# A fused attention and spectral-mix kernel: early y sums a tile sooner, a repeated x product, and moved Q jobs

## The chip, the cores and the metric

The kernel runs on one core of a Trainium2 chip. The time is device microseconds of one execution; the value given for a kernel is the median of several runs. Engines are named as in the profile: PE (TensorE matmul), PEld (its weight load), DVE (VectorE), ACT (ScalarE), POOL (GpSimd), SP (SyncE, which issues the output DMAs).

## The reference

First a causal attention with a forgetting gate, over 8 batches, 8 heads, 576 positions and 64 values per head. Its output x (8 x 576 x 512) then goes through a spectral mix with 64 modes, whose weights are by far the largest input:

```
X = rfft(x, axis=1)[:, :64]
Yr = Xr @ w_r[m] - Xi @ w_i[m]          # a 512x512 matrix for each mode m
Yi = Xr @ w_i[m] + Xi @ w_r[m]
y = irfft(Y, n=576, axis=1)
u = x + y
out = u + relu(u @ w_ch)
```

## The kernel before

The mode weights come in 64 tiles of about 1 MB (`emit_w_load`, L92), through POOL's DMA queue into a ring of nine buffers `wb` (NRING, L57). `emit_modes(n)` (L119) multiplies tile n: 32 products of 16 columns for the tiles of the second half, into a PSUM tile `A`; a DVE add (L163) then puts the sum with what the first half left in `Yacc` into `YTe` (early modes) or `YTl` (late modes). Tiles 32 to 47 hold the modes of `YTe`, the last sixteen (GL, L81) those of `YTl`.

While the weights stream, attention runs first. Then `u @ w_ch` is split: `XW = x @ w_ch` (`emit_xw`, L741) needs no mode. From tile 48 on the early half of y is complete, and is added to x and XW in 40 **parts** (a list of pairs, four for each pair of batches bp and more: one `emit_y(bp)`, L767, then nine `emit_part`, L772). `emit_y` transposes YTe of a batch pair on PE (L710), copies it on DVE (L715), multiplies it by w_ch in eight products (L718) and copies that on ACT (L726). `emit_part` forms x plus early y in `pu` and XW plus its early y in `pz` on PE (`add`, L728, four to six matmuls of 512 columns, all at L729), and evacuates them back to `x_all` and `XW`: on DVE two casts of 64 rows (L794, L795) or one whole cast (L790), on ACT two casts (L796, L797, or L792). PSUM at that time is a pool of six banks `psBig` (L737) and two for `A`.

The loop at L805 emits tile after tile, and behind each the parts that its rule at L814 makes due. `nmode` there is the number of tiles emitted, so with 15 as divisor all 40 parts are out behind tile 62, the last but one (tiles count from 0 to 63). The order in which the engines get these instructions is not quite the emitted one: the framework's scheduler places them by its own estimate, and adds the waits.

After the loop the PSUM pools are replaced by `psZ` (L820), four tiles of two banks; a tile of it waits for what used its banks before. Then the **output jobs** run (list at L881 to L885): for each pair of batches four jobs of two row blocks and one half job, 20 in all. `emit_x` (L845) puts x and XW into the job's `pu` and `pz` with products with a 64x64 identity, eight matmuls of 64x512 in the four corners of the PE array; `emit_out` (L852) adds the late y's products to them, copies `pu` on ACT (L859), and then, by the job's type, for N does relu and add in one DVE instruction (L864), for Q does the relu on ACT (L861) and the add on POOL (L862). The result goes out by a DMA from SP's queue (L874, or L870 for the half job). `emit_late(bp)` (L828) prepares the late y of a batch pair with `y_rows`, as `emit_y` does for the early one (L710, L715, L718, L726), with one psZ tile `pl`. The order is: x products of job 0, tile 63, late y of pair 0, then the jobs, with the late y of the next pair behind jobs 2, 7 and 12.

Of the kernel before, what the change touches and what calls it, by code (L numbers as in the profile page):

```python
# [11 lines left out]
ALU = mybir.AluOpType  # L12
# [9 lines left out]
def kernel(  # L22
# [11 lines left out]
    nc = tc.nc  # L34
    B, H, S, Dh = q.shape
    NM = moe_w_r.shape[0]
    D = H * Dh
# [14 lines left out]
    def xi(b, sb):  # L52
        return (b % 2) * 3 + sb if sb < 3 else 6 + b % 2 if sb == 3 else 8
# [14 lines left out]
    ident_bf = const.tile([128, 128], BF16, name="ident_bf")  # L68
# [9 lines left out]
    NT = NDC * NG  # L78
    NTH = NT // 2
    M2 = MG // 2  # L80
    GL = 16  # L81
# [92 lines left out]
    with ExitStack() as actx:  # L174
# [176 lines left out]
        for r0, n in RG:  # L351
# [7 lines left out]
            for h in range(2):  # L359
                hs = slice(h * 64, h * 64 + 64)  # L360
# [281 lines left out]
        nmode = 0  # L642

        def next_w():
            nonlocal nload
            if nload < NDC * NG:
                emit_w_load(nload)
                nload += 1
# [38 lines left out]
    with ExitStack() as bctx:  # L687
# [40 lines left out]
        def add(p, lhsT, rhs, first):  # L728
            nc.tensor.matmul(  # L729
                p, lhsT=lhsT, rhs=rhs, start=first, stop=not first, skip_group_check=True  # L730
            )

        with ExitStack() as cctx:
            late["psM"] = cctx.enter_context(
                tc.tile_pool(name="psM2", bufs=2, space=bass.MemoryType.PSUM)
            )
            psBig = cctx.enter_context(  # L737
                tc.tile_pool(name="psBig", bufs=6, space=bass.MemoryType.PSUM)
            )

            def emit_xw(n):  # L741
                bp, i0, nb = n // 2, (0, 5)[n % 2], (5, 4)[n % 2]
                xT = xTs[n % 3]
                for eb in range(NDC):
                    ptr = psBig.tile([128, SP], BF16, tag="big", name="ptr")
                    for i in range(nb):
                        nc.tensor.transpose(
                            ptr[:, i * 128 : (i + 1) * 128],
                            x_all[:, bp, i0 + i, eb * 128 : (eb + 1) * 128],
                            ident_bf[:, :],  # L750
                        )
                    nc.vector.tensor_copy(  # L752
                        xT[:, eb, 0 : nb * 128], ptr[:, 0 : nb * 128]
                    )
                for i in range(nb):
                    pxw = psBig.tile([128, D], F32, tag="big", name="pxw")
                    for eb in range(NDC):
                        nc.tensor.matmul(  # L758
                            pxw[:, :],
                            lhsT=xT[:, eb, i * 128 : (i + 1) * 128],  # L760
                            rhs=wch[:, eb, :],
                            start=(eb == 0),
                            stop=(eb == NDC - 1),
                        )
                    nc.scalar.copy(XW[:, bp, i0 + i, :], pxw[:, :])  # L765

            def emit_y(bp):  # L767
                pyw = psBig.tile([128, D], F32, tag="big", name="pyw")
                yp = psBig.tile([128, D], BF16, tag="big", name="yp")
                y_rows(YTe, 0, bp, yp[:, :], pyw[:, :])  # L770

            def emit_part(b, sb):  # L772
                pu = psBig.tile([128, D], F32, tag="big", name="pu0")
                pz = psBig.tile([128, D], F32, tag="big", name="pz0")
                bp, h = b // 2, b % 2
                xs, zs = x_all[:, bp, xi(b, sb), :], XW[:, bp, xi(b, sb), :]
                for t, (p, src) in enumerate(((pu, xs), (pz, zs))):
                    add(p[:, :], ident_bf[:, :], src, True)
                    for k in range(2 if sb == 4 else 1):
                        half = (b + k + t) % 2  # L780
                        add(
                            p[HS[k], :] if sb == 4 else p[:, :],
                            (BI if half else BIx)[
                                HS[half], sb * 128 : (512 + 64 if sb == 4 else sb * 128 + 128)
                            ],
                            yy[HS[half], 0, bp, t, :],
                            False,
                        )
                if sb == 4:
                    nc.vector.tensor_copy(xs, pu[:, :])  # L790
                    for k in range(2):
                        nc.scalar.copy(zs[HS[1 - k]], pz[HS[k], :])  # L792
                    return
                nc.vector.tensor_copy(xs[HS[h]], pu[HS[0], :])  # L794
                nc.vector.tensor_copy(zs[HS[h]], pu[HS[1], :])  # L795
                nc.scalar.copy(xs[HS[1 - h]], pz[HS[0], :])  # L796
                nc.scalar.copy(zs[HS[1 - h]], pz[HS[1], :])  # L797

            parts = []
            for bp in range(B // 2):  # L800
                parts += [(bp, None)]
                parts += [(b, sb) for b in (2 * bp, 2 * bp + 1) for sb in range(4)]
                parts += [(2 * bp, 4)]
            nx = done = 0
            while nmode < NT - 1:  # L805
                emit_modes(nmode)
                nmode += 1
                next_w()
                if nmode > NTH + 6 and nmode % 4 and nx < B:
                    emit_xw(nx)  # L810
                    nx += 1
                if nmode > NT - GL:
                    assert nx == B
                    while done < (nmode - NT + GL) * len(parts) // (GL - 1):  # L814
                        a, sb = parts[done]
                        emit_y(a) if sb is None else emit_part(a, sb)
                        done += 1
            assert done == len(parts)
# [13 lines left out]
        def pieces(job):  # L832
            b, sb, nb, _ = job
            for i in range(nb):
                at = b // 2, xi(b, sb + i)
                for k in range(2):
                    for t in range(2):
                        half = (b + t + (k if sb == 4 else 0)) % 2
                        src = (x_all, XW)[t if sb == 4 else k]
                        c0 = 512 if sb == 4 else (sb + i) * 128 + HM * k  # L840
                        yield t, i, HS[k], HS[half], src[HS[half], at[0], at[1], :], (
                            BIx if half else BI
                        )[HS[half], c0 : c0 + HM]

        def emit_x(job):  # L845
            pu = psZ.tile([128, 2, D], F32, tag="z", name="pu")
            pz = psZ.tile([128, 2, D], F32, tag="z", name="pz")
            for t, i, o, hs, src, _ in pieces(job):
                add((pu, pz)[t][o, i, :], ident_bf[hs, hs], src, True)
            return pu, pz  # L850

        def emit_out(job, ps, last):  # L852
            b, sb, nb, ty = job
            for t, i, o, hs, _, basis in pieces(job):
                add(ps[t][o, i, :], basis, yy[hs, 1, b // 2, t, :], False)
            pu, pz = (p[:, 0:nb, :] for p in ps)
            uo = wpool.tile([128, 2, 2, D], F32, tag="wb", name="uo")
            u_sb, o_sb = uo[:, 0, 0:nb, :], uo[:, 1, 0:nb, :]
            nc.scalar.copy(u_sb, pu)  # L859
            if ty == "Q":  # L860
                nc.scalar.activation(o_sb, pz, ACT.Relu)  # L861
                nc.gpsimd.tensor_tensor(o_sb, o_sb, u_sb, ALU.add)  # L862
            else:
                nc.vector.scalar_tensor_tensor(  # L864
                    o_sb, pz, 0.0, u_sb, ALU.max, ALU.add
                )
            if sb == 4:
                for h in range(2):
                    eng = nc.scalar if last and h else nc.sync
                    eng.dma_start(  # L870
                        out[b + h, 512:576, :], uo[64 * h : 64 * h + 64, 1, 0, :]
                    )
            else:
                nc.sync.dma_start(  # L874
                    out[b, 128 * sb : 128 * sb + 256, :].rearrange(
                        "(p r) e -> p r e", r=2
                    ),
                    o_sb,
                )

        jobs = []  # L881
        for bp in range(B // 2):
            jobs += [(b, sb, 2) for b in (2 * bp, 2 * bp + 1) for sb in (0, 2)]
            jobs.append((2 * bp, 4, 1))
        jobs = [(*j, ty) for j, ty in zip(jobs, "NNQNNNNQNNNNQNNNNNNN")]  # L885
        ps0 = emit_x(jobs[0])
        emit_modes(nmode)
        emit_late(0)
        for n, job in enumerate(jobs):
# [31 lines left out]
```

## Time and profile before

| | |
|---|---|
| median of 6 runs | 455.24 us (452.23 to 458.49) |
| the profiled execution | 456.33 us, its span 454.6 us |
| granted PE clock, mean over the span | 0.808 of full |
| PE busy | 384.6 us, 85% |
| DVE busy | 276.7 us, 61% |
| ACT busy | 245.7 us, 54% |
| POOL busy | 129.4 us, 28% |
| DMA | 97.02 MB, mean 213 GB/s |

The profile is of one execution. Its time is the span plus 1.7 us outside it, so times inside the span can be set against 456.33; the median of the runs shown is 1.1 us below that execution. A busy share is an average over stages with different limits, and PE also counts as busy while its matmuls run at a lower clock. All places in the profile are in us from the start of the span.

### The profile page before, as it was taken

Reading aid. Unit: us, or ns where it says so; the run is one execution under the profiler, and the core shown is the slowest. Engines: PE = TensorE matmul, PEld = TensorE weight load, DVE = VectorE, ACT = ScalarE, POOL = GpSimd, SP = SyncE. Lnnn points to the kernel's source line nnn. Section 1 sums busy time; section 2 is a strip of 40 time slices with the busy share of each in tenths; the row PEclk is TensorE's granted clock in tenths of the full one; section 3 lists DMA queues with packets and bytes.
Section 4 is the critical chain, followed back from the end, with each engine's and each line's share of the span. In section 5 each row is a group of like instructions: output and inputs, shape, how many; then the busy total and the mean of one; then the engine's idle time right before and its main releaser. Section 6 shows DMA issues by size and latency. Waiting matters only on the chain.

```text
span 454.6 us, 11981 instructions
## 1 busy us (share of the span) xinstructions
PE 384.6 (85%) x5134; PEld 247.7 (54%) x5149; DVE 276.7 (61%) x671; ACT 245.7 (54%) x372; POOL 129.4 (28%) x191
## 2 busy tenths in 40 slices
PE   2797798999887886987879886999999999979883
PEld 1464666776666565666656665666654433324341
DVE  5677778876455655555665776243359758393454
ACT  3787477774444636436446381334447764563663
POOL 7333331333323323233231213332323222000320
PEclk9996699996566858556755598899999985796998
DMA  9999999999999999999999999999999999911667
GB/s 197 222 236 260 210 255 217 222 223 212 236 211 236 236 210 237 233 214 236 234 214 211 212 210 188 209 211 211 213 210 211 211 211 211 211 20 59 244 246 286
DMA packets 49748, 97.02 MB, mean 213 GB/s; under 512 B 3296, under 2 KB 12128, under 8 KB 49696
## 3 DMA queue, kind: packets, MB, share of 16 engines
q0 software_dynamic: 46240, 85.93, 96.8%
q1 hardware_dynamic: 3376, 10.21, 6.1%
q8 instruction: 40, 0.66, 0.5%
q10 hardware_dynamic: 80, 0.13, 0.1%
q14 instruction: 12, 0.10, 0.1%
HBM read 163.73 MB, written 9.44 MB: 381 GB/s over the span
## 4 chain that ended last, share of the span: by engine, by line
PE 42%; DMA 17%; ACT 14%; DVE 11%; issue 4%; POOL 0%; ACTq 0%; DVEq 0%
DMA wb<-in_moe_w_i_dram 17%; PE pav L554 8%; ACT E L516 8%; PE A L147 7%; PE ps L509 6%; PE tp L457 5%; PE pz L729 4%; PE pu L729 3%; PE px L597 2%; DVE QTs L472 2%; PE vp L481 2%; ACT KT L470 2%; ACT uo L859 2%; DVE uo L864 2%; DVE XT L611 1%
## 5 line engine op out<-in xcount | busy, mean ns | idle before, releaser
L516 ACT ACTIVATE E<-ps 128x1024 bf16<-128x1024 f32 (+1 forms) x128 | 101.6, 854 | 29.0 <-PE ps L509 19.2
L90 POOL DMA_DIRECT2D wb<-in_moe_w_r_dram x65 | 43.3, 667 | 142.0 <-PE A L147 50.9
L147 PEld LDWEIGHTS <-wb 128*128 128x128 bf16 x2048 | 66.1, 100 | 23.2 <-issue 16.1
L147 PE MATMUL A<-XT,wb 128*128 128x16 bf16 x2048 | 73.0, 181 | 5.6 <-DVE Yacc L158 1.8
L509 PE MATMUL ps<-QTs,KT 64*128 64x64 bf16 (+4 forms) x384 | 59.0, 332 | 15.1 <-ACT E L516 13.7
L90 POOL DMA_DIRECT2D wb<-in_moe_w_i_dram x65 | 43.3, 666 | 68.7 <-DMA wb<-in_moe_w_i_dram 30.4
L554 PE MATMUL pav<-va,E 128*128 128x65 bf16 (+1 forms) x1088 | 58.2, 216 | 4.1 <-DVE x_all L576 3.5
L554 PEld LDWEIGHTS <-E 128*128 128x128 bf16 (+1 forms) x1088 | 48.0, 119 | 19.5 <-issue 8.3
L531 DVE TENSOR_TENSOR E<-E,trimask 128x256 bf16<-128x256 bf16 (+2 forms) x128 | 37.1, 301 | 19.6 <-ACT E L516 19.2
L474 ACT COPY VT<-tp 128x640 bf16<-128x640 bf16 (+1 forms) x32 | 23.3, 755 | 33.5 <-PE tp L457 33.2
L765 ACT CAST XW<-pxw 128x512 bf16<-128x512 f32 x36 | 20.8, 586 | 35.4 <-PE pxw L758 35.2
L509 PEld LDWEIGHTS <-KT 64*128 64x128 bf16 x384 | 19.5, 100 | 30.5 <-issue 21.7
L758 PE MATMUL pxw<-wch,yy 128*128 128x512 bf16 x133 | 34.1, 387 | 0.8 <-DVE yy L752 0.2
L470 ACT COPY KT<-tp 128x640 bf16<-128x640 bf16 (+1 forms) x32 | 22.1, 755 | 21.9 <-PE tp L457 21.9
L472 DVE COPY QTs<-tp 128x640 bf16<-128x640 bf16 (+1 forms) x32 | 23.2, 766 | 14.3 <-PE tp L457 14.2
L729 PEld LDWEIGHTS <-ident_bf 64*64 64x64 bf16 (+1 forms) x216 | 14.1, 104 | 32.0 <-issue 27.5
L794 DVE CAST x_all<-pu 64x512 bf16<-64x512 f32 x32 | 21.8, 682 | 15.8 <-PE pu L729 15.0
L864 DVE SCALAR_TENSOR_TENSOR uo<-pz,uo 128x1024 f32<-128x1024 f32 (+1 forms) x17 | 18.4, 1097 | 18.8 <-ACT uo L859 18.8
L576 DVE TENSOR_TENSOR x_all<-pav,rcp 128x384 bf16<-128x384 f32 x64 | 29.1, 454 | 0.8
L796 ACT CAST x_all<-pz 64x512 bf16<-64x512 f32 x32 | 18.5, 578 | 20.4 <-PE pz L729 19.0
L565 DVE RECIPROCAL rcp<-pav 128x6 f32<-128x6 f32 x64 | 12.1, 189 | 27.4 <-PE pav L554 26.4
L729 PE MATMUL pu<-x_all,ident_bf 64*64 64x512 bf16 (+1 forms) x72 | 26.2, 407 | 3.0 <-ACT uo L859 2.1
(119 smaller groups left out, 620.2 us busy)
## 6 DMA issues: line engine op xcount, KB each, us to landing
wb<-in_moe_w_r_dram POOLq DMA_DIRECT2D x63, 512.0 KB, 16.2
wb<-in_moe_w_i_dram POOLq DMA_DIRECT2D x63, 512.0 KB, 16.9
stv<-in_v_dram POOLq DMA_DIRECT2D x15, 576.0 KB, 15.1
out_dram<-uo SPq DMA_DIRECT2D x16, 512.0 KB, 2.8
stk<-in_k_dram POOLq DMA_DIRECT2D x16, 288.0 KB, 15.3
stq<-in_q_dram POOLq DMA_DIRECT2D x16, 288.0 KB, 15.2
out_dram<-uo SPq DMA_DIRECT2D x7, 128.0 KB, 3.2
stv<-in_v_dram SPq DMA_DIRECT2D x1, 576.0 KB, 4.3
```

The source lines that it names most:

```text
L90: tc.keep_in_program_order(nc.gpsimd.dma_start(dst, src))
L147: nc.tensor.matmul(A[:, eb, mi, :], lhsT=w_of(mi, eb * 128), rhs=x_of(m), start=(i == 0), stop=(i == len(terms) - 1),)
L470: nc.scalar.copy(rows(KTs[pr % 2][:, :, 0:S]), tv)
L472: nc.vector.tensor_copy(rows(QT[pr][:, :, :]), tv)
L509: nc.tensor.matmul(ps[:, b, o : o + n], lhsT=KTs[pr % 2][bs, h, jb * 128 : (jb + 1) * 128], rhs=QT[pr][bs, h, jb * 128 + c0 : jb * 128 + c ...
L516: nc.scalar.activation(E[:, :, piece * 512 : piece * 512 + w], ps[:, :, 0:w], ACT.Exp, scale=scale,)
L531: nc.vector.tensor_tensor(dg, dg, tr, ALU.mult)
L554: nc.tensor.matmul(pav[64 * half : 64 * half + w, slot, :], lhsT=E[:, b, c : c + (w - 1) * st + 1 : st], rhs=va[:, jb, b, :], start=(n == ...
L576: nc.vector.tensor_tensor(xo, pi, ri, ALU.mult)
L729: nc.tensor.matmul(p, lhsT=lhsT, rhs=rhs, start=first, stop=not first, skip_group_check=True)
L758: nc.tensor.matmul(pxw[:, :], lhsT=xT[:, eb, i * 128 : (i + 1) * 128], rhs=wch[:, eb, :], start=(eb == 0), stop=(eb == NDC - 1),)
L864: nc.vector.scalar_tensor_tensor(o_sb, pz, 0.0, u_sb, ALU.max, ALU.add)
```

## The change

Three edits and one addition. The parts rule divides by 14 instead of 15, so that all 40 parts are out behind tile 61. `emit_x` gets a count, and job 0's x product is emitted four times over into the same PSUM tiles, each time from the start. The Q jobs are 5, 10 and 15 instead of 2, 7 and 12. A new type D (relu and add on DVE straight from PSUM, without the ACT copy) is written into `emit_out`; no job in the list has it.

```diff
-                    while done < (nmode - NT + GL) * len(parts) // (GL - 1):
+                    while done < min(len(parts), (nmode - NT + GL) * len(parts) // (GL - 2)):
                         a, sb = parts[done]
                         emit_y(a) if sb is None else emit_part(a, sb)
                         done += 1
...
-        def emit_x(job):
+        def emit_x(job, times=1):
             pu = psZ.tile([128, 2, D], F32, tag="z", name="pu")
             pz = psZ.tile([128, 2, D], F32, tag="z", name="pz")
-            for t, i, o, hs, src, _ in pieces(job):
-                add((pu, pz)[t][o, i, :], ident_bf[hs, hs], src, True)
+            for _ in range(times):
+                for t, i, o, hs, src, _ in pieces(job):
+                    add((pu, pz)[t][o, i, :], ident_bf[hs, hs], src, True)
             return pu, pz
...
-            nc.scalar.copy(u_sb, pu)
-            if ty == "Q":
+            if ty != "D":
+                nc.scalar.copy(u_sb, pu)
+            if ty == "D":
+                nc.vector.scalar_tensor_tensor(o_sb, pz, 0.0, pu, ALU.max, ALU.add)
+            elif ty == "Q":
                 nc.scalar.activation(o_sb, pz, ACT.Relu)
                 nc.gpsimd.tensor_tensor(o_sb, o_sb, u_sb, ALU.add)
...
-        jobs = [(*j, ty) for j, ty in zip(jobs, "NNQNNNNQNNNNQNNNNNNN")]
-        ps0 = emit_x(jobs[0])
+        jobs = [(*j, ty) for j, ty in zip(jobs, "NNNNNQNNNNQNNNNQNNNN")]
+        ps0 = emit_x(jobs[0], 4)
         emit_modes(nmode)
         emit_late(0)
```

## The prediction

> **What bounds the kernel now.** First the page's busy tenths in 40 slices of 11.4 us, to see which stage is limited by what.
>
> ```profile
> PE   2797798999887886987879886999999999979883
> ...
> PEclk9996699996566858556755598899999985796998
> DMA  9999999999999999999999999999999999911667
> ```
>
> The DMA row is full for 35 slices: the weights set the time until the last tile lands. The windows view has 91 GB/s in 398 to 400 us and 5 GB/s after, so it lands at about 399. Yet the span is 454.6: 55 us follow, and the change works there. Next, the timeline from the fourth pair's early y to the last tile's product (start, duration, engine, line; in brackets the idle time before it and its releaser).
>
> ```profile
> 396.33 0.68 DVE L794 CAST x_all<-pu 64x512 bf16<-64x512 f32 x1 [5.00 <-PE pu L729]
> ...
> 408.52 0.69 DVE L790 CAST x_all<-pu 128x512 bf16<-128x512 f32 x1
> ...
> 408.64 0.37 PE L729 MATMUL pz<-x_all,ident_bf 64*64 64x512 bf16 x1 [2.60 <-DVE XW L795]
> ...
> 409.27 0.99 PE L147 MATMUL A<-XT,wb 128*128 128x16 bf16 x32
> ```
>
> The last tile's product starts at 409.27, ten us after its weights are there. What it waits for is DVE's queue of evacuations, unbroken from 396.33 to 409.21: eight parts at 1.44 us (two casts), two YTl adds at 0.40, one whole cast. DVE began late because PE was late, and that was the clock (columns: PE, PEld, DVE, ACT, POOL busy, granted clock, DMA share, GB/s):
>
> ```profile
> 372.00:373.00 1.00, 1.00 (x3) 0.13 (x2) 0.00 (x0) 0.63 (x2) 0.00 (x0) 0.51 1.15 215
> 392.00:393.00 1.00, 1.00 (x6) 0.11 (x2) 0.00 (x0) 0.25 (x1) 0.00 (x0) 0.75 1.13 211
> ...
> 409.00:410.00 1.00, 0.99 (x35) 0.81 (x29) 0.21 (x1) 0.00 (x0) 0.00 (x0) 0.78 0.00 0
> 416.00:417.00 1.00, 1.00 (x12) 0.60 (x8) 0.76 (x1) 0.21 (x1) 0.00 (x0) 0.80 0.00 0
> ```
>
> Read as fractions of a us, the clock halves at 372.02, returns at 392.50, halves at 409.56 and returns at 416.40: steps of 20.48, 17.06 and 6.84, which are 6, 5 and 2 times 3.41. Each fall comes 1.1 us (0.9 for the second) after a PE pause: 1.21 us for a weight tile (369.71 to 370.92), 2.6 us above. A part's matmuls then step by 0.54 us (376.38, 376.93) instead of 0.32 (345.25, 345.57).
>
> Last, ACT's timeline in one group of five output jobs, and the chain there.
>
> ```profile
> 424.62 1.01 ACT L859 COPY uo<-pu 128x1024 f32<-128x1024 f32 x1 [1.11 <-PE pz L729]
> 426.00 1.01 ACT L859 COPY uo<-pu 128x1024 f32<-128x1024 f32 x1 [0.38 <-PE pz L729]
> 428.00 1.01 ACT L859 COPY uo<-pu 128x1024 f32<-128x1024 f32 x1 [0.99 <-PE pz L729]
> 428.91 1.03 ACT L861 ACTIVATE uo<-pz 128x1024 f32<-128x1024 f32 x1
> 429.94 0.58 ACT L726 CAST yy<-pl 128x512 bf16<-128x512 f32 x1
> ```
> ```profile
> 412.31 1.85 PE pl L718 x8
> ...
> 428.91 0.98 PE pl L718 x8
> ```
>
> Jobs 5, 6 and 7 are copied at 424.62, 426.00, 428.00; 7 is the Q job, with its relu at 428.91. The group repeats every 8.96 us (422.00, 430.92, 439.93). No engine is full in it: PE, ACT and DVE hand on two pairs of PSUM tiles. The late y's eight products end at 429.89 on PE and its ACT copy starts at 429.94, as the relu ends.
>
> **The sum's base.** The profiled execution took 456.33 us (span 454.6, 1.7 around it), 1.1 above the median of six, 455.24. I work out a difference against the profiled one and apply it to the median.
>
> **1. Early y a tile sooner.** Fourteen tiles instead of fifteen carry the 40 parts: after tile 57, 28 instead of 26, after tile 61 all 40. No work is added; DVE's queue can end at most one tile time earlier, 4.95 us (the weight issues at 376.10, 381.09, 386.04), and at least 0. What delays DVE's restart at 396.33: PE idled 1.21 + 0.37 us at 370 and 375, which one more part (4 x 0.32 = 1.28) mostly fills: 1.2. By the order of the built program the fourth pair's y now stands before the products of tile 60, not after most of them: one set, 0.9 (32 at 389.88 to 390.87). The 13 products of tile 61 that stand before the first pu sum on the path, 0.31, go behind it. Taken: 2.4 sooner, from these three rows. Ends kept: 0 and 4.95.
>
> **2. The repeated x product.** It adds 24 matmuls of 64x512. Before, the x product of job 0 waited for DVE's last-but-one part and the last tile followed DVE's end by 0.06. Now the built order has its first matmul wait for the YTl add of tile 62, which stands behind all evacuations, and the last tile's 32 products, YTl of tile 63, late y and all jobs are queued on PE behind the repeats. So the repeats are not in a wait for the tile (landed at 399); they follow DVE's end. Last evacuation: 409.21 - 2.4 - 0.40 (that YTl is no longer ahead) = 406.4; YTl 0.40 and the handover 0.06: 406.9; 32 products, four at a time in 64x64 corners, 8 rounds of 0.21 (430.07, 430.28, 430.50) = 1.7, or 0.43 (411.25, 411.68) = 3.4 at half clock. The last tile's product starts at 408.6 or 410.3, against 409.27: -0.7 or +1.0.
>
> **3. The clock after it.** Half clock from 409.56 to 416.40 made late y and the first two jobs dearer: 0.61 against 0.33, 0.99 against 0.59, 1.85 against 0.98, and for the 24 products from 414.16 to 417.10 six rounds at 0.43 against 0.21, 1.3: 2.8 us together. That is the most the repeats can save; 0 is the least. PE will pause longer than before, from 403.4 (its last part ended at 405.8, less 2.4) to 406.8, against 405.8 to 408.6; so I expect the fall, and the repeats inside it, but a return one 3.41 us step sooner as dense products fill that step. Parts 2 and 3 together: between -3.5 (warm, all saved) and +1.0 (cold, nothing saved). Repeats cold and the rest warm give +1.0 - 2.8 = -1.8; repeats warm and one step saved -0.7 - 1.4 = -2.1. Taken: -1.9. The gain of 2.4 in part 1 is already in it.
>
> [...]
>
> **4. Q moved from jobs 2, 7, 12 to 5, 10, 15.** Each moves one relu on ACT (1.03), one add on POOL (2.35) and its output DMA, and puts a DVE step (1.22) in the old place. Between the copies of jobs 5 and 6 ACT idles only 0.38; a relu there pushes job 6's copy, and with it DVE's step 0.16 later and the late y behind that, by 1.03 - 0.38 = 0.65. What the old place gives back: the yy copy could start at 429.89 instead of 429.94, and in the first group it waited 0.50 for PE anyway. Three times 0.65 = +1.95. Ends: 3 x 1.03 = +3.1, and below nothing -1.5, if yy's copy came 0.5 sooner thrice. Hidden: POOL has nothing else then (idle 6.66 before an add); on SP the next job's DMA stands behind the Q job's, and its DVE step ends 1.01 + 0.03 + 1.22 = 2.26 after the relu, POOL at 2.35: 0.1 on a queue with four jobs to follow. DVE's added step lies in idle time of 3.2.
>
> The new type D is given to no job: nothing.
>
> **Sum.** -1.9 + 1.95 = 0.0 (0.05): 455.2.
>
> **Rivals.**
> Cold stretch gone (faster). If the part that fills the pause at 370 keeps the clock up, 372 to 392.5 is not slow. DVE's idle time between 388.5 and 396.33, 6.4 us, is what that stretch cost at most; taking part 1 to its end of 4.95 instead of 2.4 gives -2.5, and a warm tail -1.6 more (-3.5 for -1.9): 451.1; with all 6.4 of it 449.6. Midway 450.4. For it: the pause was 1.2 and the extra part is 1.28. Against: any pause after it can do the same, and PE's load per tile stays below the tile time.
> Repeats cold and the cold lasts (slower). Place: PE, ahead of tile 63's product. +1.0 and no tail saved, with +1.95: 455.24 + 2.95 = 458.2; with part 1 at 0, 460.6. It passes +1% when part 1 gives less than 0.8 us. For it: the longer pause. Against: the repeats are the densest work there.
> Q helps (the stated purpose). -1.5 instead of +1.95: 451.8. For it: the relu ends just as yy's copy starts. Against: PE's late y ends then too.
>
> **How the numbers follow.** Forecast 0.4, Q helps 0.15, cold stretch gone 0.2, cold repeats 0.25. A measurement of this kernel tells about 1%, 4.55 us, from no change. The forecast and Q helps lie within it; the cold stretch gone is faster; of the cold repeats 0.15 is slower, where part 1 gives less than 0.8, and 0.1 within: 0.2, 0.65, 0.15. The range runs from between the two values of the first rival, 450.4, to just short of the second's far end, 459.8; the forecast's own is 452.5 to 458.
>
> **What would show it.** Part 1: last L790 on DVE at about 406.4. Part 2: the first x product released by L163, and tile 63's product about 1.7 or 3.4 us behind it. Part 3: a halved clock before 410 and its return by 413. Part 4: a gap of 2.07 us instead of 1.38 between the first two copies of a group, and a period near 9.6 instead of 8.96. Wrong if the first x product starts before tile 62 is evacuated, if the clock never falls after 370, or if the period stays.

## The result and the profile after

| | before | after |
|---|---|---|
| median | 454.50 us (449.49 to 460.03, 65 runs) | 457.16 us (453.01 to 461.63, 28 runs) |
| ratio, 95% interval | 1 | 1.0070 [1.0048, 1.0092] |
| the profiled execution, its span | 456.33, 454.6 us | 457.0, 455.3 us |

The change makes the kernel 0.7% slower, 3.2 us (2.2 to 4.2): within the 1% that was called no change and inside the range, but slower where the forecast had no difference at all. Ratios here leave out runs more than 1.5% above the fastest of their kernel, and medians do not, so the two need not agree; differences in us are worked out from the ratios.

The page's busy tenths of the kernel after, 40 slices of 11.4 us each:

```profile
PE   2797798999887887987877887999999989969772
...
PEclk9997799996566957556759697999999985987997
DMA  9999999999999999999999999999999999903666
```

The DMA row ends as before: the last weights land near 400 us (84 GB/s from 398 to 399, 10 from 399 to 400), and all that follows is the tail the change works on. Next the timeline after (start, duration, engine, line; in brackets the idle time ahead and its releaser):

```profile
391.88 0.68 DVE L794 CAST x_all<-pu 64x512 bf16<-64x512 f32 x1 [1.07 <-PE pu L729]
...
403.79 0.69 DVE L790 CAST x_all<-pu 128x512 bf16<-128x512 f32 x1
...
404.81 0.37 PE L729 MATMUL pu<-x_all,ident_bf 64*64 64x512 bf16 x1 [3.25 <-DVE YTl L163]
...
406.71 0.63 PE L729 MATMUL pu<-x_all,ident_bf 64*64 64x512 bf16 x1
...
407.35 1.02 PE L147 MATMUL A<-XT,wb 128*128 128x16 bf16 x32
```

DVE starts its run of evacuations 4.45 us sooner (391.88 against 396.33) and ends it 4.73 sooner. Then PE stands idle 3.25 us until YTl of tile 62 releases the x product, runs it four times, and only then starts tile 63, 2.87 us behind the end of the last L790 (403.79 + 0.69); before it was 0.06. Of 4.73 us won, 1.92 arrive at tile 63. The windows after, 1 us each (PE, PEld, DVE, ACT, POOL busy, granted clock, DMA share, GB/s):

```profile
371.00:372.00 1.00, 0.78 (x3) 0.29 (x3) 0.95 (x2) 0.00 (x0) 0.00 (x0) 0.89 1.14 213
388.00:389.00 1.00, 1.00 (x9) 0.45 (x7) 0.00 (x0) 0.58 (x1) 0.00 (x0) 0.58 1.11 209
405.00:406.00 1.00, 1.00 (x24) 0.68 (x20) 0.00 (x0) 0.00 (x0) 0.00 (x0) 0.95 0.06 16
416.00:417.00 1.00, 1.00 (x19) 0.57 (x12) 0.24 (x1) 0.79 (x2) 0.00 (x0) 0.93 0.57 229
```

Read as before, the clock halves at 371.78, returns at 388.84, halves at 405.90, in the middle of the repeats, and returns at 416.14. The second cold stretch is 10.24 us, three steps of 3.41, where it was two. The first is one step shorter (17.06 for 20.48). Last, ACT's timeline in one group of output jobs:

```profile
423.24 1.01 ACT L861 COPY uo<-pu 128x1024 f32<-128x1024 f32 x1 [1.12 <-PE pz L729]
424.15 1.03 ACT L865 ACTIVATE uo<-pz 128x1024 f32<-128x1024 f32 x1
425.07 1.02 ACT L861 COPY uo<-pu 128x1024 f32<-128x1024 f32 x1
426.32 1.01 ACT L861 COPY uo<-pu 128x1024 f32<-128x1024 f32 x1 [0.23 <-PE pz L729]
429.01 0.58 ACT L726 CAST yy<-pl 128x512 bf16<-128x512 f32 x1 [1.68 <-PE pl L718]
```

The relu (L865) now stands between the first two copies, which are 1.83 us apart instead of 1.38, and the late y's copy waits 1.68 us for PE, where before it followed the relu at once. Groups start at 420.63, 429.99 and 439.45: a period of 9.36 and 9.46 for 8.92 and 9.01. And there is one row that the prediction did not read, the last output DMA on ACT's queue, in the list of DMA issues (KB, median us from issue to landing); first before, then after:

```profile
out_dram<-uo ACTq DMA_DIRECT2D x1, 128.0 KB, 3.0
```
```profile
out_dram<-uo ACTq DMA_DIRECT2D x1, 128.0 KB, 3.8
```

The spans of the two profiles differ by 0.7 us, which splits as follows, to rounding:

| stretch | before | after | difference |
|---|---|---|---|
| start to DVE's last L790 | 408.52 | 403.79 | -4.73 |
| from there to tile 63's products | 0.75 | 3.56 | +2.81 |
| tile 63's products to DVE's last output step | 41.06 | 42.89 | +1.83 |
| from there to the end of the span | 4.27 | 5.06 | +0.79 |

The chain of waits after begins only at 442.32, so the order of the groups is read from the timelines. One pair of profiles does not size the first line: over the 98 runs of the kernel before that stand beside the experiments, the time goes from 450 to 461 us, and it falls as the mean granted clock rises (correlation -0.72). The medians of the experiments size it.

### The profile page after: what moved, and what is told of

Same layout as the page of the kernel before. It is cut to its first block, busy times and chain, and to the rows that moved or that the text cites. A ratio compares the mean times of both kernels' runs of the same rounds, so it can differ in the third digit from the quotient of the medians.

```text
span 455.3 us, 12025 instructions
## 1 busy us (share of the span) xinstructions
PE 380.8 (84%) x5158; PEld 246.9 (54%) x5173; DVE 276.3 (61%) x671; ACT 245.1 (54%) x372; POOL 129.2 (28%) x191
## 3 DMA queue, kind: packets, MB, share of 16 engines
q1 hardware_dynamic: 3376, 10.21, 6.1%
## 5 line engine op out<-in xcount | busy, mean ns | idle before, releaser
L509 PE MATMUL ps<-QTs,KT 64*128 64x64 bf16 (+4 forms) x384 | 58.0, 326 | 16.2 <-ACT E L516 14.9
L554 PE MATMUL pav<-va,E 128*128 128x65 bf16 (+1 forms) x1088 | 57.1, 214 | 4.0 <-DVE x_all L576 3.4
L554 PEld LDWEIGHTS <-E 128*128 128x128 bf16 (+1 forms) x1088 | 46.9, 117 | 18.9 <-issue 8.2
L729 PE MATMUL pu<-x_all,ident_bf 64*64 64x512 bf16 (+1 forms) x78 | 29.0, 419 | 7.7 <-DVE YTl L163 3.2
L729 PE MATMUL pz<-XW,ident_bf 64*64 64x512 bf16 (+1 forms) x82 | 29.7, 421 | 0.0
```

The lines of the kernel that those rows point to most:

```text
L509: nc.tensor.matmul(ps[:, b, o : o + n], lhsT=KTs[pr % 2][bs, h, jb * 128 : (jb + 1) * 128], rhs=QT[pr][bs, h, jb * 128 + c0 : jb * 128 + c ...
L554: nc.tensor.matmul(pav[64 * half : 64 * half + w, slot, :], lhsT=E[:, b, c : c + (w - 1) * st + 1 : st], rhs=va[:, jb, b, :], start=(n == ...
L729: nc.tensor.matmul(p, lhsT=lhsT, rhs=rhs, start=first, stop=not first, skip_group_check=True)
```

## The experiments

Theory: the early parts and their earlier end help a little; the repeats cost time on the path because they stand behind DVE's queue, not in a wait, and they save none of the cold stretch; the moved relu costs about 2 us. Rivals are named at each. Ratios are to the kernel before on the same chip, with 95% intervals. "Tail" is the time from the end of tile 63's products to the end of DVE's last output step (40.07 before, 41.87 after), which is free of what came earlier.

### One edit at a time

Each edit of the change alone on the kernel before: `e1_parts_only` has the divisor, `e2_q_only` the Q jobs, `e3_repeats_only` the repeats.

```diff
-                    while done < (nmode - NT + GL) * len(parts) // (GL - 1):
+                    while done < min(len(parts), (nmode - NT + GL) * len(parts) // (GL - 2)):
```

> Early y a tile sooner, and nothing else of the change. Theory P (the terms of the prediction: parts -2.4 us, repeats and clock together +0.5, Q +1.95, of which one is too low): -2.4 us, ratio 0.995, with DVE's last evacuation (L790) some 2 to 5 us earlier and tile 63's product directly behind it. Theory R (the repeats are what costs, 2 to 3 us on PE ahead of tile 63's product, parts and Q cancel): also about -2 us. Theory N (a part sooner is worth nothing, since DVE's queue ends when it ends): ratio 1.000.

Measured: 0.9964 [0.9926, 1.0002], -1.6 us by the ratio (medians 452.98 and 454.34), with zero just inside. In its profile tile 63 starts 0.88 us behind the end of the last L790 (0.06 before), and the tail is 40.82 for 40.07: part of what is won at DVE is lost again behind it.

```diff
-        jobs = [(*j, ty) for j, ty in zip(jobs, "NNQNNNNQNNNNQNNNNNNN")]
+        jobs = [(*j, ty) for j, ty in zip(jobs, "NNNNNQNNNNQNNNNQNNNN")]
```

> Only the Q jobs moved to 5, 10, 15. Theory P: +1.95 us, ratio 1.004, with 2.07 us instead of 1.38 between the first two copies of a group on ACT and a group period near 9.6 instead of 8.96. Theory R: below +0.7 us, ratio 1.000 to 1.0015. Purpose of the edit, if it held: -1.5 us, 0.997.

Measured: 1.0058 [1.0018, 1.0097], +2.6 us. Its groups start at 421.07, 430.43 and 439.88, the periods of the kernel after, and its last DMA takes 3.8 us.

```diff
-        ps0 = emit_x(jobs[0])
+        ps0 = emit_x(jobs[0], 4)
```

> Only the x product of job 0 four times over. Its first psZ tile then waits as before for an early YTl add, the second for DVE's last-but-one part. Theory P: tile 63's product 1.1 us later (24 products, 6 rounds of 0.21, less the 0.1 it stood behind DVE), a shorter cold stretch after it: +0.5 us or less, ratio 1.000 to 1.001. Theory R: no shorter cold stretch, +1.1 at full or +2.4 at half clock, ratio 1.0025 to 1.005.

Measured: 1.0039 [0.9999, 1.0079], +1.8 us. PE's timeline of e3:

```profile
407.77 0.37 PE L729 MATMUL pz<-x_all,ident_bf 64*64 64x512 bf16 x1 [2.60 <-DVE XW L795]
...
410.46 1.02 PE L147 MATMUL A<-XT,wb 128*128 128x16 bf16 x32
```

Tile 63 now starts 2.12 us behind the end of the last L790 (407.65 + 0.69) where it was 0.06, and the clock falls at 408.70 and returns at 425.78, five steps. This execution (460.3 us) lies 5 us above the median of its kernel, so the five steps are one case and no size. That the repeats alone cost time rests on the later tile; by the ratio zero is just inside. The three single ratios add up to +0.61%; the whole change has +0.70%. So the edits add within the noise, and no interplay is needed.

### One edit left out

`e4_no_repeats` is the kernel after with the x product once, `e5_old_q` with Q at 2, 7 and 12.

```diff
-        ps0 = emit_x(jobs[0], 4)
+        ps0 = emit_x(jobs[0], 1)
```

> The changed kernel with the x product once: parts and Q moved only. Theory P: -2.4 + 1.95 = -0.45, ratio 0.999, and 0.005 to 0.006 below the changed kernel only if the repeats cost 2.5 us. Theory R: -2 us, ratio 0.995 to 0.997. If Q alone is the cost: ratio 1.004 or more, as the changed kernel has.

Measured: 0.9992 [0.9954, 1.0030]. Without the repeats the kernel after is as fast as before: they cost 0.78% here (1.0070 - 0.9992), 3.5 us, with an interval of about 1.5 to 5.5. Tile 63 starts 1.33 us behind the last L790 instead of 2.87, and the tail is 41.52 for 41.87; these two give 1.9 us. The second cold stretch is three steps either way (402.76 to 413.00 in e4). Nor does the mean granted clock of all runs rise with the repeats: it is 0.827 in the 28 runs of the kernel after for 0.832 in the 12 of e4, and 0.821 in the 12 of e3 for 0.828 in the 35 of before beside them. So four repeats at this place do not shorten the cold stretch.

```diff
-        jobs = [(*j, ty) for j, ty in zip(jobs, "NNNNNQNNNNQNNNNQNNNN")]
+        jobs = [(*j, ty) for j, ty in zip(jobs, "NNQNNNNQNNNNQNNNNNNN")]
```

> The changed kernel with the Q jobs put back to 2, 7, 12: parts a tile sooner and the x product four times. Theory P-corrected (from the single edits: parts -0.36%, repeats +0.39%, Q +0.58%, adding up): ratio 1.000. If the repeats cost more once the parts are early, since they then stand wholly behind DVE's end: 1.001 to 1.004. If Q is only dear together with the repeats: 0.997.

Measured: 1.0011 [0.9977, 1.0045]. Moving Q back wins 0.59%, 2.7 us; whether the repeats cost more once the parts are early (1.001 to 1.004) or not (1.000) this does not tell. Its profiled execution (459.45 us) lies 5 us above its median, so its profile is not used for sizes.

### The pause filled, instead of what follows it

`e6_pause_filled` is e1 with 48 products of 128 columns behind the last part, into a PSUM tile that nobody reads; `e10_before_pause_filled` has the same on the kernel before.

```diff
+            warm = late["psM"].tile([128, NDC, M2, 2 * B], F32, tag="A", name="warm")
+            for _ in range(48):
+                nc.tensor.matmul(
+                    warm[:, :, :, :], lhsT=ident_bf[:, :], rhs=ident_bf[:, :], start=True, stop=True
+                )
```

> Parts a tile sooner, old Q jobs, the x product once; in PE's pause between the last part and the x product stand 48 products of the identity with itself (128 columns, some 2.9 us) into a PSUM tile of the A pool that nobody reads and that is free before the last part is through. It adds work whose result is not used. Theory warm (the repeats fail because they stand behind the pause, not in it): the clock does not halve between 400 and 415, and the kernel is up to 2.8 us, 0.6%, below parts only: ratio 0.990 to 0.993 against before. Theory cold (filling does not hold the clock, or the fall comes later anyway): 0.996 as parts only, or above.

Measured: 0.9928 [0.9893, 0.9962], medians 450.74 and 455.34 us. PE's timeline of e6:

```profile
398.11 2.85 PE L821 MATMUL warm<-ident_bf 128*128 128x128 bf16 x48
...
401.15 0.40 PE L729 MATMUL pu<-x_all,ident_bf 64*64 64x512 bf16 x1 [0.19 <-DVE YTl L163]
...
401.71 0.96 PE L147 MATMUL A<-XT,wb 128*128 128x16 bf16 x32
```

The pause of 2.92 us in e1 shrinks to 0.19, the clock does not fall before 443.10, after the last product, and the tail is 37.85 us for e1's 40.82. So the purpose behind the repeats is sound: in this profile and the next, with work in the pause, the clock stays full from there to the end of the jobs (no fall until 443.10 and 448.94), where it fell at 403.38 in e1 and at 409.56 before. The kernel after puts it behind the pause.

> The kernel before, with 48 products of 128 columns with the identity added behind the last early part, whose result nobody uses, and nothing else changed. Theory (the pause of 2.6 us ahead of tile 63 is what halves the clock, and the cold stretch of 6.8 us behind it costs 2.8 us): no fall after 400 us, tile 63's products at about 409.3 as before, ratio about 0.994 (0.991 to 0.997). Rival (the gain of the earlier fill came from the earlier parts and the absent cold stretch at 372): the fall near 409 stays or its going gives under 1 us, ratio 0.998 to 1.002.

Measured: 0.9981 [0.9921, 1.0041], which does not tell the expected 0.994 from nothing. The effect shows in the profile: PE's timeline of e10,

```profile
404.41 2.29 PE L821 MATMUL warm<-ident_bf 128*128 128x128 bf16 x38
...
407.51 0.94 PE L147 MATMUL A<-XT,wb 128*128 128x16 bf16 x32
```

with no fall until 448.94 and a tail of 37.86, 2.2 us below that of before. Over all its 12 runs the mean granted clock is 0.840, for 0.821 in the 23 of before beside them, and the medians, 453.22 and 456.94 us, lie further apart than the ratio has it. The prediction had put the cold stretch at 2.8 us; 2.2 is what its going saves.

### Eight repeats

`e7_eight_repeats` is the kernel after with twice the repeats.

```diff
-        ps0 = emit_x(jobs[0], 4)
+        ps0 = emit_x(jobs[0], 8)
```

> The changed kernel with the x product eight times instead of four. If the repeats lie on the path: 32 more products, 8 rounds of 0.21 to 0.43, 1.7 to 3.4 us more than the changed kernel: ratio 1.011 to 1.015. If the repeats are hidden or buy the clock back: 1.007 as the changed kernel, or less, with the clock back one or two steps of 3.41 us sooner.

Measured: 1.0115 [1.0076, 1.0155], +0.45% on the change. The cold stretch is now one step (406.54 to 409.96) and the tail 39.12, 2.75 us under that of the kernel after; but tile 63 starts 5.59 us behind the end of the last L790 (404.79 + 0.69, 411.07), 2.72 more than after. With eight repeats the clock is back sooner (mean granted clock 0.840 in its six runs, 0.827 in the 28 of the kernel after), and they cost what that brings. The 1.9 us by which its profile is longer are the last DMA, which takes 4.5 us here, and a last L790 that starts 1.00 later; neither was traced to the repeats.

### No Q at all

`e9_no_q` is the kernel before with all jobs of type N.

```diff
-        jobs = [(*j, ty) for j, ty in zip(jobs, "NNQNNNNQNNNNQNNNNNNN")]
+        jobs = [(*j, ty) for j, ty in zip(jobs, "NNNNNNNNNNNNNNNNNNNN")]
```

> The kernel before with all 20 jobs N: no relu on ACT and no add on POOL anywhere, three more DVE steps of 1.22 us. Theory (the moved relu costs because it stands between the first two copies of a group; in its old place ahead of the late y's copy it was free and gave nothing): within 0.3% of before, ratio 0.998 to 1.003, group period 8.9 to 9.0 us. Rival (the old place relieved DVE, and what the move costs is that loss): as slow as the move alone, ratio 1.004 to 1.008, period 9.3 or more.

Measured: 0.9982 [0.9935, 1.0028], groups at 417.64, 426.56 and 435.57, the periods of before to 0.01, and a last DMA of 3.0 us. Two copies of ACT's timeline in e9:

```profile
420.25 1.01 ACT L861 COPY uo<-pu 128x1024 f32<-128x1024 f32 x1 [1.12 <-PE pz L729]
421.64 1.01 ACT L861 COPY uo<-pu 128x1024 f32<-128x1024 f32 x1 [0.38 <-PE pz L729]
```

They are 1.39 apart, 1.38 before. In its old place the Q job neither costs nor gives anything that the profile shows; the cost of the move is the relu between the copies, not the loss of the old place.

### Parts sooner still, and the repeats in a real wait

`e8_two_tiles_sooner` has divisor 13, the x product once and Q in the old places.

```diff
-                    while done < min(len(parts), (nmode - NT + GL) * len(parts) // (GL - 2)):
+                    while done < min(len(parts), (nmode - NT + GL) * len(parts) // (GL - 3)):
```

> Parts two tiles sooner (divisor 13), old Q jobs, the x product once. If DVE's end moves with the parts: some 1.6 us less than parts only, ratio 0.993. If DVE or PE is full over the sixteen tiles already: 0.996 as parts only, or above.

Measured: 0.9937 [0.9905, 0.9970]. Last L790 at 399.95, but the clock is halved from 384.80 to 418.92, ten steps, and the tail is 42.79.

`e12_two_tiles_filled` adds 48 products to it; here `warm` (again read by nobody) is a tile of psBig, so that it waits for ACT only.

```diff
+            _, warm = [psBig.tile([128, D], F32, tag="big", name=w) for w in ("w0", "warm")]
+            for _ in range(48):
+                nc.tensor.matmul(
+                    warm[:, 0:128], lhsT=ident_bf[:, :], rhs=ident_bf[:, :], start=True, stop=True
+                )
```

> Parts two tiles sooner than before's kernel (divisor 13), Q jobs in their old places, x product once, and the same 48 products (their result is not used) into a bank that waits for an evacuation by ACT only. Theory (early parts and a filled pause add up): last evacuation by DVE near 400, no fall between it and the jobs, ratio 0.986 to 0.990, at or below the 0.993 of divisor 14 with the pause filled. Rival (the cold stretch that begins near 385 in this denser stage lasts through the filled pause): ratio 0.992 to 0.996 as without the fill.

Measured: 0.9855 [0.9787, 0.9922], the theory's size, but half of the rival's way to it. The cold stretch (385.00 to 405.48) does last into the fill: at half clock the 48 products take 4.72 us instead of 2.85 and hold tile 63 until 406.85 (403.51 in e8), 3.3 us later. Behind them the clock is full and the tail 37.85, 4.9 us shorter.

`e11_three_tiles_filled` has the same fill and divisor 12.

```diff
-                    while done < min(len(parts), (nmode - NT + GL) * len(parts) // (GL - 3)):
+                    while done < min(len(parts), (nmode - NT + GL) * len(parts) // (GL - 4)):
```

> Parts three tiles sooner than before's kernel (divisor 12), Q jobs in their old places, x product once, and 48 products with the identity behind the last part into a bank that waits for an evacuation by ACT only (their result is not used). If DVE's queue still sets tile 63, its last evacuation comes below 399 us, tile 63 follows the landing of its weights at about 399 to 401, and the ratio is 0.985 to 0.990. If a long half-clock stretch in the denser stage before it takes that back, the ratio is 0.993 or more and the profile shows more than five steps of 3.41 us at half clock after 380 us.

Measured: 0.9808 [0.9744, 0.9873], 446.81 us, better than the 0.985 to 0.990 of the first case, which its interval just reaches; last L790 at 393.72. One line of PE's timeline in e11:

```profile
400.23 0.54 PE L147 MATMUL A<-XT,wb 128*128 128x16 bf16 x14 [1.04 <-DMA wb<-in_moe_w_i_dram]
```

For the first time tile 63 waits for its weights, no longer for DVE. And that makes the wait in which the change meant to put its repeats.

`e15_three_tiles_alone` is e11 without the 48 products.

```diff
-            _, warm = [psBig.tile([128, D], F32, tag="big", name=w) for w in ("w0", "warm")]
-            for _ in range(48):
-                nc.tensor.matmul(
-                    warm[:, 0:128], lhsT=ident_bf[:, :], rhs=ident_bf[:, :], start=True, stop=True
-                )
```

> Parts three tiles sooner (divisor 12), Q in the old places, x product once, without the 48 products. If the gain of the filled kernel is the earlier parts alone (its own clock fell at 399.60 in spite of the 48 products), the ratio is 0.979 to 0.983 and the last tile still starts at the landing, 400.2. If the 48 products carry it, a fall comes before 399.6 or lasts past 406.4, and the ratio is 0.985 to 0.99.

Measured: 0.9887 [0.9841, 0.9933], above the 0.983 that earlier parts alone were to give, with the clock halved from 397.50 to 414.56 and a tail of 42.77 for e11's 39.85: by the clock it is the second case, in which the 48 products carry a part. The two ratios overlap and come from two chips, so they do not size that part.

What stayed open was whether repeats in four corners of 64x64 fail by their place or by their form. `e13_three_tiles_repeats4` and `e14_three_tiles_repeats8` are e11 with the x product four and eight times.

```diff
-        ps0 = emit_x(jobs[0], 1)
+        ps0 = emit_x(jobs[0], 4)
```

> The kernel with parts three tiles sooner and the 48 products (divisor 12, Q in the old places), with job 0's x product four times. There, with the x product once, PE waits 0.41, 0.71 and 1.04 us for the last tile's weights between 396.8 and 400.2 and the clock falls at 399.60. Theory (the repeats of the change failed by their place behind DVE's queue): here three more rounds of 0.43 us lie in the wait, tile 63's last products still start with the weights at about 400.2, so they cost nothing (under 0.3 us). They end near 398, before the last wait of 1.04 us, so the fall may stay: ratio 0.976 to 0.982. Rival (repeats in four corners of 64x64 do not keep the clock wherever they stand, and delay the tile): tile 63 later by 1 us or more, fall stays, ratio 0.983 or more.

Measured: 0.9852 [0.9811, 0.9892], 445.97 us. PE's timeline of e13, and of e15 below it, which has neither repeats nor fill:

```profile
396.92 0.37 PE L729 MATMUL pu<-x_all,ident_bf 64*64 64x512 bf16 x1 [0.46 <-DVE YTl L163]
...
398.43 0.38 PE L729 MATMUL pu<-x_all,ident_bf 64*64 64x512 bf16 x1
...
398.77 0.61 PE L147 MATMUL A<-XT,wb 128*128 128x16 bf16 x18
400.30 0.51 PE L147 MATMUL A<-XT,wb 128*128 128x16 bf16 x14 [0.92 <-DMA wb<-in_moe_w_i_dram]
```
```profile
396.09 0.94 PE L147 MATMUL A<-XT,wb 128*128 128x16 bf16 x32 [2.59 <-DVE YTl L163]
397.49 0.58 PE L729 MATMUL pu<-x_all,ident_bf 64*64 64x512 bf16 x1 [0.46 <-DVE YTl L163]
...
399.58 0.55 PE L147 MATMUL A<-XT,wb 128*128 128x16 bf16 x14 [0.44 <-DMA wb<-in_moe_w_i_dram]
```

The eight rounds end at 398.8, and the last weights still set tile 63 (400.30; 400.23 in e11): the repeats cost nothing, as the theory had it. Its ratio missed the theory's 0.976 to 0.982, which was counted from e11's 0.9808 on another chip; by e15 beside it, 0.9887, e13 is 0.35% better, which the 48 products and the repeats share. The windows of e13 show a fall at 401.16 and a return at 404.58, one step, against two in e11, which has the 48 products alone, and five in e15:

```profile
401.00:402.00 1.00, 0.74 (x6) 0.53 (x8) 0.30 (x2) 0.00 (x0) 0.00 (x0) 0.58 0.00 0
404.00:405.00 1.00, 1.00 (x8) 0.24 (x6) 0.00 (x0) 0.25 (x1) 0.00 (x0) 0.71 0.00 0
```

> The same with the x product eight times: 16 rounds of 0.21 us, 3.4 in all, from 396.6 to 400.0, so that PE is busy until the last weights land. Theory (place): no fall near 399.6, tile 63's products end at about 401.0 instead of 400.8, the late y of pair 1 comes 1.7 to 2 us sooner behind it, ratio 0.975 to 0.979. Rival (form): the clock falls at 399.6 as with one, or the tile is 1 us late; ratio 0.982 or more.

Measured: 0.9860 [0.9816, 0.9903], 446.12 us. By its ratio and its late tile this is what the rival expected, but not by its cause. No fall comes until 441.16, and the tail is 37.85: behind eight repeats of this form the clock stays full, in this profile. But the x product began later than in e11 (398.38 for 396.59, DVE's last L790 at 395.95 for 393.72), and the 3.4 us of repeats then ran past the landing, so that tile 63 started at 401.96 and ended at 402.92, 2.11 us after e13's. They save 1.48 us of tail against e13. Of the 2.11 us, 1.46 is the later start of the x product (398.38 for 396.92 in e13), which came ahead of any repeat; so what the four further repeats cost at the tile is less than they save, and the ratios do not tell e14 from e13. So the form is not what failed: in a real wait four repeats are free (e13's tile 63). That it is they who shorten the cold stretch from two steps to one is one profile against another.

The ratios of e11, e13 and e14 overlap, and only the profiles tell them apart; that all three are faster than before is beyond their intervals. e13 has the lowest median, 445.97 us, and beats both kernels.

## Why the prediction was wrong

**Part 1, early y.** Mechanism right, size within the ends. The last L790 ended at 404.48, not 406.4: 4.7 us sooner in this pair, where 2.4 and 0.40 were taken and 4.95 was the most. A cold stretch of 17.06 us for 20.48 is in it. The pause read as 1.21 us was 1.01: the row at 369.71 lasts 0.20, and the next has `[1.01 <-DMA wb<-in_moe_w_i_dram]`. Over the profiles of five kernels with divisor 15 (before, e2, e3, e9, e10) the last L790 starts at 406.7 on average, over six with 14 (after, e1, e4 to e7) at 403.0: 3.6 sooner. By the ratio e1 has -1.6 us (-3.4 to +0.1): about 0.8 is lost again at tile 63 (a lag that the prediction counts in part 2) and 0.75 in a longer cold tail, which it did not count. The sign "first x product released by L163" held: 404.81.

**Part 2, the repeats' place.** Right, sharply: they follow DVE's end. Between the start of YTl and tile 63 lie 0.41 and 2.54 us, the latter between the 1.7 (warm) and 3.4 (cold) of the prediction, since the clock falls in the middle of them.

**Part 3, the clock: the step that failed.** The prediction took "a return one 3.41 us step sooner as dense products fill that step", and with it -1.9 for parts 2 and 3. The return was to come by 413; it came at 416.14, after three steps, and by e4 the repeats do not change that number. The forecast for the repeats was +0.5 us (-1.9 with part 1's -2.4 in it); the runs have +1.8 (e3, 0.0 to 3.6) to +3.5 us (after against e4, about 1.5 to 5.5): they cost their time on the path and bought nothing back. The other two terms measure -1.6 for -2.4 (parts) and +2.6 for +1.95 (Q), both within the noise of their runs. The rival "repeats cold and the cold lasts", given 0.25, was the one that came true in kind: +2.95 us worked out, +3.2 measured. That the sums lie so close is in part luck: in the profiles tile 63 starts 1.92 us sooner, where the rival had it 1.0 later, and a longer tail and a later last DMA make up for it. The price of the cold tail was a little high: 2.8 predicted, 2.2 by the tail of before against e10.

That dense products bring the return sooner, the term behind the -1.9, was the author's estimate: no row of before shows it, and after and e4 have three steps each, with the x product four times and once. Nor does a busy PE bring the return by itself: in e3 PE is busy for all 6.00 us from 417 to 423, a whole step of the grid with it (418.94 to 422.35), at half clock throughout, and the clock returns at 425.78 only. The prediction read each fall as coming about 1 us behind a pause of PE. A pause does stand ahead of each of these: 1.01 us before, 0.92 and 0.25 us (ending at 369.88 and 371.22) ahead of the fall at 371.78 after, and 3.25 us ahead of the one at 405.90. But the length of the pause does not decide it: in e1 PE waits 1.57 us for a weight tile, to 386.05, and the clock does not fall before 403.38. So no length of pause that is enough for a fall can be read from these rows.

**Part 4, Q.** Mechanism right, size right by two errors. Predicted 3 x 0.65 = 1.95; e2 measures 2.6 us (0.8 to 4.4), and after against e5 2.7. In the profile the second copy is pushed by 0.45, not 0.65: relu and copy each start 0.10 before the instruction ahead of them ends (424.15 against 423.24 + 1.01), which the prediction's subtraction of durations left out. The groups cost 0.44, 0.45 and 0.39 more, 1.28 together; e7's tail, with no cold stretch behind tile 63, is 1.27 above the 37.85 of such kernels with Q in its old places. To this comes the last DMA: 3.8 us for 3.0 in after, e2 and e4 (4.5 in e7), 3.0 or 3.1 in all kernels with Q in its old places or without it; 0.8 us that the prediction had booked as "0.1 on a queue". That makes 2.1, within the interval of e2. The windows show what the DMA engines carry by then, first before, then after (DMA share and GB/s are the last two columns):

```profile
448.00:449.00 1.00, 0.62 (x5) 0.14 (x4) 0.83 (x2) 0.42 (x1) 0.00 (x0) 1.00 0.46 184
```
```profile
446.00:447.00 1.00, 0.74 (x14) 0.52 (x15) 0.93 (x2) 0.24 (x1) 0.48 (x1) 1.00 0.00 0
448.00:449.00 1.00, 0.17 (x2) 0.00 (x0) 0.58 (x1) 0.87 (x2) 0.00 (x0) 1.00 1.02 410
```

Before, the DMA engines are half idle shortly ahead of the last issue (450.36). After, DVE's last output steps come in pairs, no output moves from 445 to 447, four SP issues stand close together from 446.51 on, and the engines are full from 448 to 453; the last DMA is issued at 450.27, into full engines. In e2 and e4 the engines are likewise idle (a share of 0.02 from 446 to 447, 0.00 from 444 to 445) and then full until the last issue (450.70, 448.09); in e3, e5 and e9, as before, one less loaded window (0.41, 0.56, 0.28; 0.46 before) comes about 2 us ahead of it. That this backlog makes the 0.8 us is the author's reading. "Q helps" has fallen.

**Rivals left.** "Cold stretch gone" did not come in the kernel after (halved from 371.78); the extra part did not fill the pause, of which 0.92 us for a weight tile remained. All five profiles with divisor 15 have a stretch of 20.48 us between 350 and 393 us; of the six with 14, three have one of 17.06 (after, e4, e5), one of 23.89 (e7), and e1 and e6 have none. Each is one execution, so what the change does to its frequency stays open.

## What to carry to other kernels

Work added to keep a clock up belongs inside the pause (48 products there took 2.2 us off the tail in e10): before adding it, find what releases its first instruction and what is queued behind it; if it is released by what ends the pause, it lies on the path (the four repeats cost 3.5 us by e4 and saved no step). Move the wait first (here the parts, until the weights and not DVE set the last tile), then fill it (in e13 four repeats cost nothing: tile 63 at 400.30 for 400.23). In a chain of copies, an instruction added to an engine that is busy for 54% of the span still costs what it pushes between two steps of the chain (here the second copy by 0.45 us), and its outputs have to be followed to the last DMA (3.8 us for 3.0).

## What the runs showed of the chip

In each profile the changes of the clock lie on a grid of 3.41 us (before and after over the whole span, the experiments from 340 us on; e6 and e14 have only one change there). The cold stretches last one to ten steps, from 3.42 us in e7 and e13 to 34.12 in e8.

The price of a cold stretch, in kernels with Q in its old places or without Q, by how long the clock stays halved behind the end of tile 63's products:

| kernel | half clock behind tile 63, us | tail, us |
|---|---|---|
| e6, e10, e12, e14 | 0 | 37.85, 37.86, 37.85, 37.85 |
| e13 | 3.42 (401.16 to 404.58) | 39.33 |
| e11 | 5.67 (400.77 to 406.44) | 39.85 |
| before | 6.14 (410.26 to 416.40) | 40.07 |
| e1, e9 | 10.11, 10.21 | 40.82, 40.87 |
| e3, e8, e15 | 14.30, 14.39, 14.43 | 42.78, 42.79, 42.77 |

Kernels that agree in the first column within 0.2 us agree in the second within 0.1, though they differ in all else; a us at half clock costs between 0.29 and 0.43 us of tail. What decides the return is open: e13 and e15 run the same kinds of products in the steps that end at 404.58 and 404.33, and the first gets its clock back there, the second ten us later.
